# LayerNorm of the first query blocks on the finished residual tiles, with its modulation sums and the down-projection preparation in other slots

## The chip, the cores and the metric

The kernel runs on one core of a Trainium2 chip. The metric is the device time of one execution in microseconds. The core has a matrix engine (TensorE, PE in the profile; PEld is its weight load), VectorE (DVE), ScalarE (ACT), GpSimd (POOL), and SyncE (SP), which issues nearly all DMAs of this kernel from one queue in program order.

## The reference

A transformer block with modulation from a condition vector `c`, for 2048 rows of 512 features; 32 query heads, 8 key and value heads of 128, a window of the last 512 cached positions.

```
mod = silu(c) @ w_mod                     # six rows: sa, ca, ga, sb, cb, gb
h = layernorm(x) * (1 + ca) + sa
x = x + ga * attention(h, k_cache, v_cache, wq, wo)
h = layernorm(x) * (1 + cb) + sb
x = x + gb * ((gelu(h @ w_gate) * (h @ w_up)) @ w_down)
```

The change concerns the second `layernorm` (with `cb` and `sb`) for the first 1024 of the 2048 rows, that is for eight tiles of 128 rows.

## The kernel before

All matrix products are done in float16 with each operand split into a high and a low part, so one product is three matmuls (`mm3`, lines 86 to 88). The rows are cut into 16 tiles of 128, four tiles make a query block of 512, and two blocks make a half. A first stage of 512 steps does the attention: half 0 (blocks 0 and 1) in steps 0 to 255, half 1 in steps 256 to 511. A step takes one tile of one head: the scores (`scores`), the row maximum on VectorE (`peak`, L899), the exponential on ScalarE (`expo`, L908), and, two and three steps later, the high part on ScalarE (`high`, L920) and the low part on VectorE (`low`, L925), which SP then transposes by DMA into `pt`. Two PSUM banks hold the scores, so the scores of a step need the exponential of the step two before. Between the scores of two steps TensorE does three groups of other products from a list: query projections, probabilities times values (`po`), and the output projection (`py`), which VectorE adds into the residual tile `acc` (L876). After step 511 a second stage does the gated feed-forward part.

Everything else is hung on this loop by step numbers. `at(t, fn)` runs a function at the end of step t, `at(("w", t), fn)` after the loads of that step; `sched(pos, (load, steps))` plans a load three steps ahead of its first use and the steps at their slots. Loads planned so share five buffers of the tag `raw` in turn, which a planner at the end of the function counts through; `spare` moves planned loads and stores into steps without a DMA. Instructions of one engine run in the order in which the steps record them.

When a tile of half 0 has got its last output projection (`attn_final`, L882), the tile is stored to DRAM as `y1`, and three steps later its buffer is loaded with a tile of half 1. The second LayerNorm of the first eight tiles is generation 2 of `ln_tile` (L444): it is planned by `plan_gen(2, ...)` at steps 288, 299, 315, 326, 342, 353, 369 and 380. It reloads the tile from `y1` into a raw buffer (`xs`), takes mean and variance on VectorE (`bn_stats`, L376), a power on GpSimd (L386), normalizes on VectorE (L458), transposes on TensorE (L463), applies scale and shift on ScalarE (L471) into a tile `hf` from the six buffers `e` that the exponentials also use, stores it, and splits it into high (ScalarE, L483) and low (GpSimd, L485). Generation 3 (the other eight tiles) does the same in the second stage.

Scale and shift come from the modulation. For each of the six rows and four groups of 128 features, `mod_load` loads a 128x512 tile of weights (`wmc`) and `mod_col` forms one sum on VectorE (L135). Rows 3 and 4 are summed at slots 257 to 271, row 5 at slots 274 to 286; `mod_max` and `mod_scale` then turn rows 3 and 4 into scaled columns, at steps 272 and 274.

From step 286 on, every 27 steps, `prep_set` and `prep_wd` (L1262, L1301) prepare two sets of gate and up weights and two tiles of down-projection weights for the second stage: loaded, scaled and split on GpSimd into `stage` tiles (raw buffers too) and stored back. `prep_wd` starts 18 steps into each period.

Of the kernel before, what the change touches and what calls it, by code (L numbers as in the profile page):

```python
# [17 lines left out]
P = 128  # L18
# [45 lines left out]
def block_kernel(ctx: ExitStack, tc: tile.TileContext, x, kT, v, wq, wo, wg, wu, wd, cT, wc, wm, out):  # L64
# [379 lines left out]
    def ln_tile(gen, i, src):  # L444
        jsc, jsh = ln_cols("a" if gen < 2 else "f")
        qb, i = divmod(i % (2 * QT), QT)
        st = {}

        def load():
            st["x"] = raw("xs")  # L450
            dma(st["x"], src())

        def stat():
            ln_stat(st["x"], st)
            ln_power(st)

        def norm():
            nc.vector.tensor_scalar(st["x"], st["x"], st["mv"][:, 0:1], st["rs"], op0=ALU.subtract, op1=ALU.mult)  # L458

        def turn():  # L460
            st["ps"] = bank("acc", "pln", NACC)
            for dt in range(KT):
                nc.tensor.transpose(st["ps"][:, dt * P:(dt + 1) * P], st["x"][:, dt * P:(dt + 1) * P], ident)  # L463

        def affine(dts):
            if 0 in dts:
                st["f"] = tmp("hf")
            f = st["f"]
            for dt in dts:
                sl = slice(dt * P, (dt + 1) * P)  # L470
                nc.scalar.activation(f[:, sl], st["ps"][:, sl], AF.Identity,  # L471
                                     scale=cols[:, jsc, dt:dt + 1], bias=cols[:, jsh, dt:dt + 1])
            if KT - 1 in dts:
                dma(spilled(gen, qb)[:, :, i * P:(i + 1) * P], f.rearrange("p (k q) -> p k q", k=KT))

        def parts(act):
            o = slice(i * P, (i + 1) * P)
            f = st["f"].rearrange("p (k q) -> p k q", k=KT)
            for h, name in enumerate(("b11", "b21") if qb == 0 else (None, "b22")):
                if name:  # L480
                    t, src = block(gen, name), f[:, 2 * h:2 * h + 2, :]
                    if act:
                        nc.scalar.activation(t[:, 0:2, o], src, AF.Copy)  # L483
                    else:
                        nc.gpsimd.tensor_tensor(t[:, 2:4, o], src, t[:, 0:2, o], op=ALU.subtract)  # L485

        more = [lambda: parts(True), lambda: parts(False)] if gen < 3 else []
        return load, [stat, norm, turn, lambda: affine((0, 1)), lambda: affine((2, 3))] + more
# [393 lines left out]
    def attn_final(ti):  # L882
        y1[ti] = dram.tile([P, D], F32, name=f"y{ti}")
        dma(y1[ti], acc[ti])
        nxt = (ti + 2 * QT) % NT
        at(now[0] + 3, lambda: load_acc(nxt, rows_of(x, nxt) if ti < 2 * QT else y1[nxt]))

    def scores(t):
        u, i = divmod(t, 4)
# [188 lines left out]
    for dt in range(KT):  # L1078
        sched(6 + dt, (lambda dt=dt: gate_load(dt), [lambda dt=dt: gate_cols(dt)]), ahead=8)
    at(("d", 10), lambda: ts(cols[:, 2, :], gps["ps"][:, 0:KT], 1.0, None, ALU.mult))  # L1080
    for j, ts_ in ((3, (257, 261, 265, 269)), (4, (259, 263, 267, 271)), (5, (274, 278, 282, 286))):
        for dt in range(KT):
            box = {}
            sched(ts_[dt], (lambda box=box, j=j, dt=dt: box.update(f=mod_load(j, dt)), [lambda box=box: box["f"]()]))
    at(11, lambda: mod_row(2))
    mx = {}
    at(("w", 272), lambda: mx.update(m=mod_max(3)))
    at(274, lambda: mod_scale(3, "mf", 1.0, mx["m"]))

    def sched_combos(gen, p, base):  # L1090
        for k, (load, steps) in enumerate(combos(gen, p, nc.gpsimd if gen or p == 0 else nc.vector, False, 0 if gen else 1 if p else 2, 0 if gen or p else 5)):
# [18 lines left out]
            sched_combos(gen, p, t_cb + dcb * p)  # L1110

    plan_gen(1, [78 + 16 * i for i in range(8)], 201, 33, lambda i: rows_of(x, 2 * QT + i))
    plan_gen(2, [T // 2 + 32 + 27 * (i // 2) + 11 * (i % 2) for i in range(8)], 478, 10, lambda i: y1[i])

    def store_set(key, k):
        store(("w", key, k), SET[key][k])
# [214 lines left out]
    for n in range(NP):  # L1331
        b = T // 2 + 30 + 27 * n
        prep_set(2 * n, b)
        prep_set(2 * n + 1, b + 13)
        prep_wd(n, b + 18)
    for k in range(2):
        at(T - 1 + 2 * k, lambda k=k: WO.update({("f", 0, k): fetch(("wd", 0, k), get_wo())}))
    for q, ps_ in ((0, (T - 18, T - 17, T - 16, T - 15)), (1, (T - 8, T - 7, T - 3, T)), (2, (T + 2, T + 3, T + 4, T + 5))):
# [228 lines left out]
```

## Time and profile before

| | us |
|---|---|
| median of three runs | 1769.49 |
| lowest, highest | 1769.39, 1770.97 |
| the profiled execution | 1767.57 |
| its span, first to last instruction | 1765.8 |
| TensorE busy | 1730.5 |
| VectorE busy | 1442.3 |
| ScalarE busy | 1210.3 |
| GpSimd busy | 875.9 |

The granted TensorE clock was 1.000 over the span. Rows of the timeline give the start in us, the length, the engine, the line, the operation, output and inputs, and in brackets how long the engine stood idle before it and what ended that. Rows by stretch give the stretch, its length, and then busy time and number of instructions for PE, PEld, DVE, ACT and POOL, the granted clock, the busy share of the DMA engines and GB/s. Rows of a tile give the count and the shortest, median and longest duration in ns, with the start of the first and the last in us. Rows of groups give busy time in us and the mean in ns, then the idle time of the engine before them. Rows of waits give the sum in us, how often, and the longest.

### The profile page before, as it was taken

The numbers are of one execution on the slowest core, as the hardware profiler recorded it, in microseconds if no ns is written. First come the engines' busy times: TensorE is split into PE (matmuls) and PEld (weight loads), VectorE is DVE, ScalarE is ACT, GpSimd is POOL, SyncE is SP. The second block draws the span as 40 slices with busy tenths as digits, with TensorE's granted clock in tenths as the row PEclk, the third lists the DMA queues.
The fourth block names the chain that finished last, engine by engine and source line by source line (L and its number), as shares of the span: only waits on it lengthen the run. The fifth ranks groups of instructions, "written<-read, shape, count | busy, mean of one in ns | idle before, by whom it ended". The sixth has DMA issues, their size and how long they took to land.

```text
span 1765.8 us, 25953 instructions
## 1 busy us (share of the span) xinstructions
PE 1730.5 (98%) x8112; PEld 796.0 (45%) x8114; DVE 1442.3 (82%) x2517; ACT 1210.3 (69%) x2814; POOL 875.9 (50%) x1095
## 2 busy tenths in 40 slices
PE   7899999999999999999999999999999999999999
PEld 5444444444444444444444444444444444444443
DVE  7888888888888888988888888888885867766676
ACT  6887787878778777677878777777773455434342
POOL 4879878776788872235475465565520033000000
PEclk9999999999999999999999999999999999999999
DMA  7999998999999989998999999999985543252222
GB/s 230 211 196 212 214 217 200 223 203 219 217 217 229 205 186 196 205 225 200 236 205 219 234 214 200 223 207 208 198 171 141 182 146 111 69 188 75 86 75 75
DMA packets 663273, 329.71 MB, mean 187 GB/s; under 512 B 553184, under 2 KB 575968, under 8 KB 663136
## 3 DMA queue, kind: packets, MB, share of 16 engines
q1 hardware_dynamic: 662848, 327.53, 80.2%
q8 instruction: 64, 1.05, 0.2%
q14 instruction: 73, 0.60, 0.1%
q10 hardware_dynamic: 288, 0.52, 0.1%
HBM read 133.83 MB, written 59.90 MB: 110 GB/s over the span
## 4 chain that ended last, share of the span: by engine, by line
PE 76%; DVE 11%; ACT 5%; POOL 3%; issue 3%; DMA 2%; SPq 0%; POOLq 0%; ACTq 0%; DVEq 0%
PE py L86 7%; PE py L87 7%; PE py L88 7%; PE ps L86 5%; PE ps L88 5%; PE ps L87 5%; PE po L86 4%; PE po L87 4%; PE po L88 4%; DVE p L925 3%; PE fa L86 3%; PE fa L88 2%; PE fa L87 2%; DVE nm L899 2%; PE qa L86 2%
## 5 line engine op out<-in xcount | busy, mean ns | idle before, releaser
L908 ACT ACTIVATE ee<-ps,nm 128x512 f32<-128x512 f32 x512 | 351.2, 686 | 254.1 <-DVE nm L899 244.4
L925 DVE SCALAR_TENSOR_TENSOR p<-ee,rr,p 128x512 f16<-128x512 f32 x512 | 463.4, 905 | 0.2
L899 DVE TENSOR_REDUCE nm<-ps 128x1 f32<-128x512 f32 x512 | 348.8, 681 | 73.5 <-PE ps L88 72.0
L920 ACT ACTIVATE p<-ee,rr 128x512 f16<-128x512 f32 x512 | 365.2, 714 | 1.7 <-DMA pt<-p 1.4
L86 PE MATMUL ps<-k,qt 128*128 128x512 f16 x512 | 194.1, 379 | 16.5 <-DVE qt L668 13.1
L86 PE MATMUL py<-wo,ot 128*128 128x512 f16 x512 | 194.1, 379 | 1.6 <-DVE ot L668 1.6
L86 PE MATMUL po<-pt,v 128*128 128x512 f16 x512 | 194.1, 379 | 0.1
L87 PE MATMUL po<-pt,v 128*128 128x512 f16 x512 | 194.0, 379 | 0.0
L88 PE MATMUL po<-pt,v 128*128 128x512 f16 x512 | 194.0, 379 | 0.0
L87 PE MATMUL py<-wo,ot 128*128 128x512 f16 x512 | 194.0, 379 | 0.0
L88 PE MATMUL py<-wo,ot 128*128 128x512 f16 x512 | 194.0, 379 | 0.0
L88 PE MATMUL ps<-k,qt 128*128 128x512 f16 x512 | 194.0, 379 | 0.0
L87 PE MATMUL ps<-k,qt 128*128 128x512 f16 x512 | 193.9, 379 | 0.0
L916 DVE RECIPROCAL rr<-rr 128x2 f32<-128x2 f32 x256 | 41.5, 162 | 102.7 <-ACT rr L913 101.3
L386 POOL TENSOR_TENSOR rs<-rs,nhalf 128x1 f32<-128x1 f32 x32 | 19.6, 611 | 194.1 <-DVE rs L380 191.5
L86 PEld LDWEIGHTS <-w 128*128 128x128 f16 x728 | 71.2, 98 | 88.4 <-DMA w<-kept 2.9
L87 PEld LDWEIGHTS <-w 128*128 128x128 f16 x728 | 71.2, 98 | 87.3 <-issue 2.7
L88 PEld LDWEIGHTS <-w 128*128 128x128 f16 x728 | 71.2, 98 | 86.0 <-issue 0.2
L876 DVE SCALAR_TENSOR_TENSOR acc<-py,dysc,acc 128x512 f32<-128x512 f32 x112 | 81.6, 746 | 28.8 <-PE py L88 28.0
L876 DVE SCALAR_TENSOR_TENSOR acc<-py,ysc,acc 128x512 f32<-128x512 f32 x128 | 94.6, 739 | 10.9 <-PE py L88 10.9
L908 ACT ACTIVATION_READ_ACCUMULATOR ee<-ps,nm 128x1 f32 x512 | 100.7, 197 | 0.0
L668 DVE SCALAR_TENSOR_TENSOR ot<-po,ot 128x512 f16<-128x512 f32 x128 | 86.9, 679 | 0.0
(263 smaller groups left out, 3817.1 us busy)
## 6 DMA issues: line engine op xcount, KB each, us to landing
w<-kept SPq DMA_DIRECT2D x123, 256.0 KB, 3.2
wo<-kept SPq DMA_DIRECT2D x60, 256.0 KB, 3.6
raw<-in_wo SPq DMA_DIRECT2D x56, 256.0 KB, 3.2
kept<-stage SPq DMA_DIRECT2D x56, 256.0 KB, 3.4
kept<-w SPq DMA_DIRECT2D x39, 256.0 KB, 3.4
rw<-in_wq SPq DMA_DIRECT2D x38, 256.0 KB, 3.3
hs<-hf SPq DMA_DIRECT2D x32, 256.0 KB, 2.7
pt<-p SPq DMA_TRANSPOSE x512, 3.5
```

Source lines behind the costliest of these rows:

```text
L86: nc.tensor.matmul(ps, llo, rhi, start=first, stop=False, skip_group_check=chain)
L87: nc.tensor.matmul(ps, lhi, rlo, start=False, stop=False, skip_group_check=chain)
L88: nc.tensor.matmul(ps, lhi, rhi, start=False, stop=last, skip_group_check=chain)
L386: nc.gpsimd.tensor_tensor(st["rs"], st["rs"], nhalf, op=ALU.pow)
L668: return lambda: nc.vector.scalar_tensor_tensor(t[:, 1, :], src, scale, t[:, 0, :], op0=ALU.mult, op1=ALU.subtract)
L876: nc.vector.scalar_tensor_tensor(acc[ti], st["p"], by, acc[ti], op0=ALU.mult, op1=ALU.add)
L899: nc.vector.tensor_reduce(nm, E[t]["ps"], axis=AX.X, op=ALU.max, negate=True)
L908: nc.scalar.activation(e, E[t]["ps"], AF.Exp, bias=E[t]["nm"], scale=1.0, accum_out=sm[:, t % 2:t % 2 + 1])
L916: return lambda: nc.vector.reciprocal(r, r)
L920: nc.scalar.activation(p16[:, 0, :], E[t]["e"], AF.Copy, scale=E[t]["r"])
L925: nc.vector.scalar_tensor_tensor(p16[:, 1, :], E[t]["e"], E[t]["r"], p16[:, 0, :], op0=ALU.mult, op1=ALU.subtract)
```

## The change

For generation 2, `ln_tile` works on the residual tile itself: no reload, the statistics are taken from `acc`, GpSimd forms minus mean times the reciprocal deviation (`nmean`), and the norm is one ScalarE activation in place where it was a VectorE operation. `hf` is taken from the raw buffers, without being known to the planner. The steps hang on `attn_final`: statistics one step after a tile is finished, norm six, transposes eight, scale and shift nine and ten, parts twelve and thirteen steps after. The load of the next tile into the same buffer moves from three to twelve steps after. The sums of rows 3 and 4 move to slots 211 to 229, and their maximum and scale to steps 232 and 234. `prep_wd` starts 21 steps into each period where it was 18. The combinations of generation 2 stay at steps 478 and 488.

```diff
--- before.py
+++ after.py
@@ -447,14 +447,22 @@
         st = {}
 
         def load():
-            st["x"] = raw("xs")
-            dma(st["x"], src())
+            if gen == 2:
+                st["x"] = src()
+            else:
+                st["x"] = raw("xs")
+                dma(st["x"], src())
 
         def stat():
             ln_stat(st["x"], st)
             ln_power(st)
+            if gen == 2:
+                st["nm"] = small.tile([P, 1], F32, name="nmean")
+                pool_ts(st["nm"], st["mv"][:, 0:1], st["rs"], -1.0)
 
         def norm():
+            if gen == 2:
+                return nc.scalar.activation(st["x"], st["x"], AF.Identity, bias=st["nm"], scale=st["rs"])
             nc.vector.tensor_scalar(st["x"], st["x"], st["mv"][:, 0:1], st["rs"], op0=ALU.subtract, op1=ALU.mult)
 
         def turn():
@@ -464,7 +472,7 @@
 
         def affine(dts):
             if 0 in dts:
-                st["f"] = tmp("hf")
+                st["f"] = raw("hf") if gen == 2 else tmp("hf")
             f = st["f"]
             for dt in dts:
                 sl = slice(dt * P, (dt + 1) * P)
@@ -883,7 +891,14 @@
         y1[ti] = dram.tile([P, D], F32, name=f"y{ti}")
         dma(y1[ti], acc[ti])
         nxt = (ti + 2 * QT) % NT
-        at(now[0] + 3, lambda: load_acc(nxt, rows_of(x, nxt) if ti < 2 * QT else y1[nxt]))
+        if ti < 2 * QT:
+            own, steps = ln_tile(2, ti, lambda: acc[ti])
+            own()
+            for d, fn in zip((1, 6, 8, 9, 10, 12, 13), steps):
+                at(("w", now[0] + d), fn)
+            at(now[0] + 12, lambda: load_acc(nxt, rows_of(x, nxt)))
+        else:
+            at(now[0] + 3, lambda: load_acc(nxt, y1[nxt]))
 
     def scores(t):
         u, i = divmod(t, 4)
@@ -1078,14 +1093,14 @@
     for dt in range(KT):
         sched(6 + dt, (lambda dt=dt: gate_load(dt), [lambda dt=dt: gate_cols(dt)]), ahead=8)
     at(("d", 10), lambda: ts(cols[:, 2, :], gps["ps"][:, 0:KT], 1.0, None, ALU.mult))
-    for j, ts_ in ((3, (257, 261, 265, 269)), (4, (259, 263, 267, 271)), (5, (274, 278, 282, 286))):
+    for j, ts_ in ((3, (211, 215, 223, 227)), (4, (213, 217, 225, 229)), (5, (274, 278, 282, 286))):
         for dt in range(KT):
             box = {}
             sched(ts_[dt], (lambda box=box, j=j, dt=dt: box.update(f=mod_load(j, dt)), [lambda box=box: box["f"]()]))
     at(11, lambda: mod_row(2))
     mx = {}
-    at(("w", 272), lambda: mx.update(m=mod_max(3)))
-    at(274, lambda: mod_scale(3, "mf", 1.0, mx["m"]))
+    at(("w", 232), lambda: mx.update(m=mod_max(3)))
+    at(234, lambda: mod_scale(3, "mf", 1.0, mx["m"]))
 
     def sched_combos(gen, p, base):
         for k, (load, steps) in enumerate(combos(gen, p, nc.gpsimd if gen or p == 0 else nc.vector, False, 0 if gen else 1 if p else 2, 0 if gen or p else 5)):
@@ -1110,7 +1125,8 @@
             sched_combos(gen, p, t_cb + dcb * p)
 
     plan_gen(1, [78 + 16 * i for i in range(8)], 201, 33, lambda i: rows_of(x, 2 * QT + i))
-    plan_gen(2, [T // 2 + 32 + 27 * (i // 2) + 11 * (i % 2) for i in range(8)], 478, 10, lambda i: y1[i])
+    for p in range(2):
+        sched_combos(2, p, 478 + 10 * p)
 
     def store_set(key, k):
         store(("w", key, k), SET[key][k])
@@ -1332,7 +1348,7 @@
         b = T // 2 + 30 + 27 * n
         prep_set(2 * n, b)
         prep_set(2 * n + 1, b + 13)
-        prep_wd(n, b + 18)
+        prep_wd(n, b + 21)
     for k in range(2):
         at(T - 1 + 2 * k, lambda k=k: WO.update({("f", 0, k): fetch(("wd", 0, k), get_wo())}))
     for q, ps_ in ((0, (T - 18, T - 17, T - 16, T - 15)), (1, (T - 8, T - 7, T - 3, T)), (2, (T + 2, T + 3, T + 4, T + 5))):
```

## The prediction

> **What bounds the kernel now.** I read the page first, then the busy time by stretches, then in order of time the places where TensorE stands still.
>
> ```profile
> span 1765.8 us, 25953 instructions
> PE 1730.5 (98%) x8112; PEld 796.0 (45%) x8114; DVE 1442.3 (82%) x2517; ACT 1210.3 (69%) x2814; POOL 875.9 (50%) x1095
> PE 76%; DVE 11%; ACT 5%; POOL 3%; issue 3%; DMA 2%; SPq 0%; POOLq 0%; ACTq 0%; DVEq 0%
> ```
>
> TensorE works 98% of the span and carries 76% of the chain that ended last. The change neither adds nor removes a matmul or a transpose, so only TensorE's idle time can change. The rows below give, by stretch, the length and then the busy time of PE, PEld, DVE, ACT and POOL.
>
> ```profile
> 560.00:620.00 60.00, 59.45 (x279) 26.77 (x277) 50.35 (x92) 46.53 (x116) 53.12 (x70) 1.00 0.97 213
> 640.00:650.00 10.00, 9.37 (x44) 4.12 (x43) 8.44 (x12) 6.51 (x17) 6.40 (x7) 1.00 0.75 179
> 680.00:720.00 40.00, 40.00 (x187) 18.09 (x186) 37.67 (x75) 28.56 (x68) 7.39 (x8) 1.00 0.94 211
> 720.00:740.00 20.00, 18.97 (x89) 8.67 (x88) 18.37 (x34) 12.75 (x31) 11.73 (x14) 1.00 0.84 177
> 740.00:790.00 50.00, 50.00 (x238) 23.25 (x237) 43.40 (x83) 38.63 (x94) 14.86 (x20) 1.00 1.00 226
> 820.00:840.00 20.00, 19.10 (x89) 8.15 (x87) 18.05 (x33) 14.56 (x37) 16.10 (x20) 1.00 0.87 204
> 870.00:890.00 20.00, 20.00 (x98) 9.39 (x97) 17.42 (x34) 17.59 (x44) 10.26 (x15) 1.00 1.03 220
> 900.00:910.00 10.00, 9.19 (x44) 4.01 (x42) 8.29 (x15) 6.94 (x17) 6.70 (x7) 1.00 1.02 255
> 970.00:980.00 10.00, 9.00 (x44) 4.01 (x42) 8.73 (x16) 5.92 (x16) 5.67 (x6) 1.00 1.00 238
> 1010.00:1260.00 250.00, 250.00 (x1172) 113.69 (x1171) 209.48 (x366) 191.43 (x465) 144.05 (x183) 1.00 0.98 212
> ...
> 500.00:1300.00 800.00, 794.26 (x3716) 361.43 (x3714) 687.62 (x1211) 613.76 (x1491) 464.38 (x565) 1.00 0.96 212
> ```
>
> Between 500 and 1300 us, where everything is that the change touches, TensorE idles only 800.00 - 794.26 = 5.74 us. That caps any gain here at 0.32% of the span. The idle time stands in few places: 0.55 us (560:620), 0.63 (640:650), 1.03 (720:740), 0.90 (820:840), 0.81 (900:910) and 1.00 (970:980). VectorE is 94% busy in 680:720 and TensorE still has no gap there, so a full engine is not a stop by itself; a late row maximum is. The next rows show the stop at 732 us and those at 908 and 977.
>
> ```profile
> 727.17 0.38 PE L194 MATMUL pst<-ident,mm 128*128 128x128 f32 x2
> 728.59 0.41 DVE L196 TENSOR_REDUCE mg<-pst 128x2 f32<-128x256 f32 x1
> 730.31 0.68 DVE L135 SCALAR_TENSOR_TENSOR wmc<-wmc,sbc 128x512 f32<-128x512 f32 x1
> 730.92 0.68 DVE L899 TENSOR_REDUCE nm<-ps 128x1 f32<-128x512 f32 x1
> 731.63 0.69 ACT L908 ACTIVATE ee<-ps,nm 128x512 f32<-128x512 f32 x1 [4.09 <-DVE nm L899]
> 732.46 0.38 PE L86 MATMUL ps<-k,qt 128*128 128x512 f16 x1 [1.03 <-ACT ee L908]
> ...
> 906.00 0.67 DVE L376 BATCH_NORM_STATS2 bn<-xs 128x6 f32<-128x512 f32 x1
> 907.71 0.69 ACT L908 ACTIVATE ee<-ps,nm 128x512 f32<-128x512 f32 x1 [2.66 <-DVE nm L899]
> ...
> 974.84 0.69 DVE L376 BATCH_NORM_STATS2 bn<-xs 128x6 f32<-128x512 f32 x1 [1.20 <-DMA xs<-y]
> ```
>
> At 728 the scale of the modulation (mod_scale) and a modulation sum stand on VectorE ahead of the maximum nm; the exponential comes late, its score bank is not free, and TensorE loses 1.03 us. At 906 and 975 the LayerNorm statistics of a reloaded tile take that place, the second time after 1.20 us of waiting for the reload.
>
> **The change part by part.** The profiled execution took 1767.57 us, its span and 1.77 us around it; the median of the runs is 1769.49, 1.92 above it. The sum goes against 1767.57 and the 1.92 are added at its end. These rows place and price the moved work.
>
> ```profile
> L135 DVE SCALAR_TENSOR_TENSOR wmc<-wmc,sbc x12: 676/682/1093, 684.6 to 758.6; 128x512 f32<-128x512 f32 x12
> DMA to landing us min/median/max: 2.9/3.3/4.6
> ...
> L94 SPq DMA_DIRECT2D y<-acc x16: 319/529/643, 688.7 to 1370.9; - x16
> L405 ACT ACTIVATE xn<-acc,nmean x2: 721/722/722, 7.7 to 8.7; 128x512 f32<-128x512 f32 x2
> ...
> L376 DVE BATCH_NORM_STATS2 bn<-xs x24: 660/680/695, 228.8 to 1429.6; 128x6 f32<-128x512 f32 x24
> L458 DVE TENSOR_SCALAR xs<-xs,mv,rs x24: 533/540/548, 235.7 to 1431.9; 128x512 f32<-128x512 f32 x24
> L94 SPq DMA_DIRECT2D xs<-y x16: 331/406/646, 758.0 to 1426.3; - x16
> ...
> 779.47 0.81 ACT L471 ACTIVATE hf<-pln,cols 128x128 f32<-128x128 f32 x2
> 782.38 0.81 ACT L471 ACTIVATE hf<-pln,cols 128x128 f32<-128x128 f32 x2
> 784.44 0.73 ACT L483 ACTIVATE b<-hf 128x256 f16<-128x256 f32 x2
> ...
> L386 POOL TENSOR_TENSOR rs<-rs,nhalf 128x1 f32<-128x1 f32 x32 | 19.6, 611 | 194.1 <-DVE rs L380 191.5 <-DVE nmean L383 2.6
> ```
>
> The twelve sums run at steps 257 to 286 and lie between 684.6 and 758.6 us, so a step is about 2.55 us; slots 211 to 229 are about 567 to 613 us, slot 234 about 626.
>
> 1. *LayerNorm taken out of 758 to 1000 us.* Eight reloads of 256 KB, eight statistics, norms, transposes and affines leave this region, and a landing can no longer hold VectorE. The three stops fall away: 0.90 + 0.81 + 1.00 = 2.71 us. The reason to expect all of it: the down-projection tiles are prepared every 27 steps (69 us) and go on after the LayerNorm has ended, and in 1010:1260 TensorE has 250.00 busy of 250.00. If the stops belong to that preparation alone, the gain is 0.
>
> 2. *mod_scale from step 274 to 234.* The 1.03 us at 732 go. At 234 the same chain runs with no sum behind it (0.68 us less), so it costs at least about 1.03 - 0.68 = 0.35; the combinations of the second query blocks begin beside it and 640:650 already has 0.63 idle, so at most 1.03 + 0.63 = 1.66. I take 1.0: the same chain, the neighbouring row.
>
> 3. *Eight sums at 567 to 613 us.* Each is 0.68 us on VectorE when GpSimd rests, 1.09 in the one case that met it; eight are 5.4 to 8.7 us. VectorE has 60.00 - 50.35 = 9.65 us idle in 560:620, so they fit, but leave 1.0 to 4.2. The lower price is 0 (680:720 holds 94% with no gap); the upper is one stop like the one at 732 for each group of four, 2.06. I take 0.8, below the middle, because 680:720 is the same instruction at the same spacing. Their loads go out three steps ahead (7.6 us) and land in 2.9 to 4.6, as before.
>
> The port is where a page speaks against this. The row has twelve sums with a median of 682 ns and one of 1093, and that one, the first at 684.6 us, is the one beside GpSimd work. The Trainium skill, page "SBUF — State Buffer", section "Who interferes with whom", says that a VectorE instruction with two SBUF inputs contends with a GpSimd instruction that reads SBUF, and that the later one waits out the earlier. The trace agrees: 1093 against 682. By that rule all eight sums would take the long price in 560:620, where GpSimd is 53.12 of 60 busy; that is the second rival below.
>
> 4. *LayerNorm in place at 689 to 793 us.* The finished tiles appear about every four steps (10.2 us) from 688.7 on, so eight LayerNorms now follow each other where they stood 11 to 16 steps apart. ScalarE gets per tile 0.81 + 0.81 + 0.73 from the rows, and the norm, which VectorE did in 0.54; the nearest ScalarE row is L405, the same shape from the same tile, 0.72. That is 3.07 per tile, 2.7 with the one high part of the second block. Over 680 to 790 ScalarE is 28.56 + 12.75 + 38.63 = 79.94 busy of 110; seven tiles more (one lies there already) bring about 21 us: 101 of 110, 92%. VectorE was 37.67 + 18.37 + 43.40 = 99.44; it loses eight sums and mod_scale (about 7.5) and gains about seven statistics of 1.0, so it stays. GpSimd gets eight small products (each under the 0.61 of its power) and the low parts, and is only 33.98 of 110 busy; its weight sets now queue behind each tile's statistics. Nothing in SP's queue waits longer: each store follows its affine as before, and the loads of the next x tiles, nine steps later, are first needed at about step 290.
> Bounds: 0 from the tile at 764 to 786, which ran without a gap in 740:790, and from 870:890, where ScalarE has 17.59 of 20 and TensorE 20.00; above, every tile stops TensorE as long as the dearer of those at 900 and 820, 8 x 0.90 = 7.2. I take 0.1 per tile, 0.8, since the nearest rows show none and this load is only somewhat higher.
>
> 5. *hf in the five raw buffers, and the preparation three slots later.* 0: with the reloads gone the raw queue has eight tenants fewer and eight other ones. What hides it is the lead of the transposed probabilities over their use; the longest such hold now is this one.
>
> ```profile
> SPq L94 <- POOL stage L157: 29.8, 15, 3.8
> ```
>
> SP stood up to 3.8 us behind GpSimd fifteen times in 780:1260, and TensorE never waited for a transpose. If that cover is gone, a stop costs about 1 us, the price of the others here.
>
> Sum: 1767.57 - 2.71 - 1.03 + 1.0 + 0.8 + 0.8 = 1766.4 profiled, and + 1.92 = **1768.4 us** as a median. With the lower ends, -2.71 - 1.03 + 0.35 = -3.4: 1766.1. With the upper ends, -3.74 + 1.66 + 2.06 + 7.2 = +7.2: 1776.7; without the gain of step 1, 2.7 more.
>
> **The rivals.**
>
> *ScalarE becomes the bound from 700 to 790 us (slower).* Eight tiles in a row at 92% leave no time to catch up, exponentials come late as at 732, and each tile costs 0.90: -1.1 + 6.4 = +5.3, so 1774.8. For it: 900:910 stops with ScalarE at only 6.94 of 10. Against it: 870:890. It decides where a tile's four steps hold more ScalarE work than 10.2 us; the base of 79.94 / 110 x 10.2 = 7.4 plus 3.07 is 10.5, a little over, though adjoining rows overlap by about 0.1 us each, which makes the true need smaller.
>
> *The sums meet GpSimd (slower).* At 1.09 each VectorE is at 50.35 + 8.7 = 59.1 of 60; if none of that finds idle time, 8.7 takes the place of 0.8: +6.8, so 1776.2. It decides when VectorE's idle time there, mostly waits for scores, is really the lead of TensorE. Against it: 680:720.
>
> *The stops belong to the down-projection preparation.* They stay at 820, 900 and 970: +2.7, so 1771.1. Against it: 1010:1260.
>
> *Both new places are free (faster).* The lower ends, and the reshuffled order also takes the 0.55 and 0.63 of 560:650: -4.6, so 1764.9.
>
> **How the numbers follow.** What a measurement of this kernel tells from no change is about 0.2%, 3.5 us; the bounds are 1765.95 and 1773.03. My forecast has 0.45, with its own range 1766.0 to 1771.0; the stops that stay 0.14 (within the bound too); ScalarE the bound 0.15; the sums on GpSimd 0.09; the free case 0.17. So faster 0.17, same 0.59, slower 0.24. The range of 1764.8 to 1774.8 takes in the free case and the middle of the ScalarE case and leaves out about 0.17, nearly all above.
>
> **What would show it.** Right: no reload of y tiles before 1300 us; no gap at 820 to 980; TensorE idle in 500:1300 between 3.5 and 6; eight LayerNorms between 689 and 793 with ScalarE near 92%; the sums at 567 to 613 above 0.68 us where GpSimd works. Wrong: scores waiting for ee in 700:790 by more than 2 us in sum, sums followed by late maxima at 567 to 626, or TensorE waiting for pt. The end beyond 1300 us should be the same; a difference there would be one that I have no step for.

## The result, and the profile after

The changed kernel took 1775.83 us (median of 6 runs, 1774.93 to 1778.80) beside 1769.68 us for the kernel before in the same series: 1.0035 times as long, 95% interval 1.0025 to 1.0046. A second series (the last experiment) gave 1.0027 (1.0018 to 1.0036). The prediction was 1768.4 us and no change.

The profiled execution took 1774.93 us. Its page begins with the span, the busy time of each engine and the chain that ended last:

```profile
span 1773.1 us, 25974 instructions
PE 1734.3 (98%) x8114; PEld 796.1 (45%) x8114; DVE 1449.5 (82%) x2509; ACT 1215.7 (69%) x2822; POOL 877.8 (50%) x1103
PE 70%; DVE 14%; ACT 8%; issue 3%; DMA 2%; POOL 2%; SPq 0%; ACTq 0%; POOLq 0%; DVEq 0%
```

The chain gave 6 points of TensorE away, three each to VectorE and ScalarE. Where, the table by stretch shows. The columns are the length, then busy time (and instructions) of PE, PEld, DVE, ACT and POOL, the granted clock, the DMA share and GB/s. First the changed kernel:

```profile
560.00:640.00 80.00, 76.24 (x353) 33.89 (x351) 74.38 (x140) 58.23 (x142) 65.07 (x79) 1.00 0.97 219
640.00:660.00 20.00, 18.16 (x85) 8.08 (x84) 17.09 (x26) 15.45 (x38) 14.34 (x14) 1.00 0.85 213
690.00:740.00 50.00, 50.00 (x240) 23.46 (x238) 43.81 (x80) 39.21 (x94) 19.95 (x26) 1.00 0.88 191
740.00:800.00 60.00, 57.46 (x278) 27.21 (x277) 49.53 (x96) 53.12 (x132) 27.05 (x37) 1.00 0.92 201
800.00:1010.00 210.00, 210.00 (x983) 95.28 (x982) 182.76 (x309) 160.71 (x390) 116.92 (x151) 1.00 0.96 212
...
500.00:1300.00 800.00, 789.50 (x3692) 358.98 (x3691) 691.38 (x1197) 614.99 (x1489) 467.63 (x576) 1.00 0.95 208
```

and the same stretches of the kernel before, in the same view:

```profile
560.00:640.00 80.00, 79.44 (x371) 35.80 (x369) 68.33 (x120) 62.04 (x152) 68.30 (x82) 1.00 0.98 212
640.00:660.00 20.00, 19.37 (x90) 8.61 (x89) 17.89 (x27) 14.20 (x35) 15.67 (x17) 1.00 0.83 168
690.00:740.00 50.00, 48.97 (x228) 22.25 (x227) 46.63 (x94) 34.99 (x82) 12.81 (x14) 1.00 0.93 201
740.00:800.00 60.00, 60.00 (x284) 27.76 (x283) 52.67 (x101) 46.94 (x115) 16.58 (x22) 1.00 1.02 233
800.00:1010.00 210.00, 207.29 (x976) 94.88 (x975) 179.87 (x320) 164.14 (x405) 124.42 (x162) 1.00 0.96 217
```

TensorE's idle time rose by 3.20 us in 560:640 (0.56 to 3.76) and by 1.21 in 640:660, fell by 1.03 in 690:740, rose by 2.54 in 740:800, and fell by 2.71 in 800:1010. Over 500:1300 it went from 5.74 to 10.50 us. Behind each rise stand single stops of TensorE. The longest, in the timeline of the changed kernel, with start and duration of each, with the idle time ahead of it and what ended that in brackets:

```profile
603.59 1.62 DVE L135 SCALAR_TENSOR_TENSOR wmc<-wmc,sbc 128x512 f32<-128x512 f32 x1
605.82 1.66 DVE L940 SCALAR_TENSOR_TENSOR p<-ee,rr,p 128x512 f16<-128x512 f32 x1
608.13 0.39 PE L86 MATMUL py<-wo,ot 128*128 128x512 f16 x1 [1.70 <-DVE ot L676]
656.40 0.39 PE L86 MATMUL ps<-k,qt 128*128 128x512 f16 x1 [1.84 <-DVE qt L676]
746.74 0.66 PE L471 MATMUL pln<-ident,acc 128*128 128x128 f32 x4 [0.80 <-ACT hf L479]
774.72 0.81 ACT L479 ACTIVATE hf<-pln,cols 128x128 f32<-128x128 f32 x2
775.65 0.17 DVE L931 RECIPROCAL rr<-rr 128x2 f32<-128x2 f32 x1 [1.44 <-ACT rr L928]
777.13 0.39 PE L86 MATMUL py<-wo,ot 128*128 128x512 f16 x1 [1.01 <-DVE ot L676]
791.23 0.66 PE L471 MATMUL pln<-ident,acc 128*128 128x128 f32 x4 [0.73 <-ACT hf L479]
1278.30 0.39 PE L86 MATMUL ps<-k,qt 128*128 128x512 f16 x1 [1.58 <-DVE qt L676]
```

A sum takes 1.62 us instead of 0.68 and the low half of the probabilities behind it 1.66. Behind both on VectorE stands `ot`, the attention result that the output projection (`py`) needs, and it comes 1.70 us late. At 656 (step 242) `qt`, the queries of the next scores, is late. At 747 and 791 the transposes of a LayerNorm tile wait for the affine (the scale and shift that write `hf`) of the tile before. At 777 `ot` is late again: on ScalarE an affine stands ahead of the softmax factor `rr`, and VectorE waits 1.44 us for it. At 1278 (step 486) `qt` is late. In the kernel before, the stops answering those at 656 and 1278 are short:

```profile
648.16 0.39 PE L86 MATMUL ps<-k,qt 128*128 128x512 f16 x1 [0.63 <-DVE qt L668]
...
1270.87 0.39 PE L86 MATMUL ps<-k,qt 128*128 128x512 f16 x1 [0.20 <-DVE qt L668]
```

**A part that is not the change.** The profiled spans differ by 7.3 us, but 2.4 of that is there by 200 us, where both kernels run the same program. The changed kernel's profile has a low granted clock in two places (rows of the columns as above, PE alone: length, busy, clock, DMA share, GB/s):

```profile
66.00:68.00 2.00, 0.89 (x4) 0.97 0.17 36
68.00:70.00 2.00, 2.00 (x6) 0.50 1.08 259
70.00:72.00 2.00, 2.00 (x9) 0.68 0.84 202
...
86.00:88.00 2.00, 0.14 (x1) 1.00 1.07 185
88.00:90.00 2.00, 2.00 (x7) 0.59 1.02 240
90.00:92.00 2.00, 2.00 (x7) 0.56 0.25 94
```

The kernel before has 1.00 in all of these stretches in its profile. Whether that belongs to the change is taken up below. Without it the traces differ by about 5 us, and the named terms add up to 3.20 + 1.21 - 1.03 + 2.54 - 2.71 + 1.38 (the stop at 1278, 1.58 against 0.20) = **+4.6 us**, a ratio of 1.0026, inside both intervals. About 0.3 us stays unnamed.

### The profile page after: what moved, and what is told of

Read it like the earlier page. It is cut to its first block, busy times and chain, and to the rows that moved or that the text cites. A ratio compares the mean times of both kernels' runs of the same rounds, so it can differ in the third digit from the quotient of the medians.

```text
span 1773.1 us, 25974 instructions
## 1 busy us (share of the span) xinstructions
PE 1734.3 (98%) x8114; PEld 796.1 (45%) x8114; DVE 1449.5 (82%) x2509; ACT 1215.7 (69%) x2822; POOL 877.8 (50%) x1103
## 3 DMA queue, kind: packets, MB, share of 16 engines
q8 instruction: 64, 1.05, 0.3%
## 4 chain that ended last, share of the span: by engine, by line
PE 70%; DVE 14%; ACT 8%; issue 3%; DMA 2%; POOL 2%; SPq 0%; ACTq 0%; POOLq 0%; DVEq 0%
PE py L86 7%; PE py L87 7%; PE py L88 7%; DVE p L940 4%; PE ps L86 4%; PE ps L88 4%; PE ps L87 4%; PE po L86 4%; PE po L88 4%; PE po L87 4%; DVE nm L914 3%; PE fa L86 3%; PE fa L88 2%; PE fa L87 2%; ACT ee L923 2%
## 5 line engine op out<-in xcount | busy, mean ns | idle before, releaser
L940 DVE SCALAR_TENSOR_TENSOR p<-ee,rr,p 128x512 f16<-128x512 f32 x512 | 469.3, 917 | 0.8 <-ACT p L935 0.7
```

Source lines behind the costliest of these rows:

```text
L940: nc.vector.scalar_tensor_tensor(p16[:, 1, :], E[t]["e"], E[t]["r"], p16[:, 0, :], op0=ALU.mult, op1=ALU.subtract)
```

## The experiments

Theory 1: the sums beside a busy GpSimd, and the LayerNorm in dense order, make the loss; its rivals are given with each run. The diffs are in short form, each with the kernel that it starts from. "Idle" is TensorE's idle time from the table by stretch in 560:640, 640:660 and 690:800: before 0.56, 0.63, 1.03; changed 3.76, 1.84, 2.54. Ratios are to the kernel before in the same series. The expectations reckon a stop from the starts of the matmuls, which makes it about 0.17 us longer than the brackets of the rows (1.43 for 1.26).

| run | median us | ratio (95%) | idle |
|---|---|---|---|
| e1_sums_only | 1773.99 | 1.0022 (1.0013-1.0031) | 3.63, 1.62, 0.12 |
| e2_sums_quiet | 1770.33 | 1.0000 (0.9991-1.0009) | 0.87, 0.63, 3.02 |
| e3_wd18 | 1773.56 | 1.0019 (1.0010-1.0028) | 4.04, 1.73, 2.57 |
| e4_one_input | 1770.72 | 1.0002 (0.9993-1.0011) | 1.48, 1.86, 2.57 |
| e5_dve_alone | 1772.65 | 1.0011 (1.0002-1.0019) | 2.08, 0.64, 3.42 |
| e6_loads_alone | 1768.10 | 0.9988 (0.9979-0.9997) | 0.82, 0.64, 3.09 |
| e7_spaced_wd18 | 1779.40 | 1.0052 (1.0039-1.0065) | 0.28, 0.65, 8.46 |
| e8_norm_dve | 1771.05 | 1.0004 (0.9995-1.0013) | 0.59, 0.64, 4.19 |
| e9_scale_late | 1774.30 | 1.0026 (1.0015-1.0036) | 3.80, 0.76, 2.82 |
| e10_quiet_wd18 | 1768.39 | 0.9991 (0.9982-1.0000) | 0.36, 0.68, 3.04 |
| e11_turn_late | 1773.26 | 1.0020 (1.0010-1.0030) | 0.63, 0.64, 5.59 |
| e12_hf_tmp | 1769.21 | 0.9995 (0.9986-1.0004) | 0.34, 0.64, 3.04 |
| e13_affine_x | 1769.20 | 0.9992 (0.9983-1.0000) | 0.25, 0.64, 2.23 |
| e14_affine_once | 1768.72 | 0.9994 (0.9985-1.0002) | 0.61, 0.64, 1.96 |
| e15_affine_once6 | 1769.48 | 0.9992 (0.9982-1.0001) | 0.75, 0.64, 1.63 |
| e16_after_again | 1775.06 | 1.0027 (1.0018-1.0036) | 4.26, 1.85, 2.53 |

e16 is the changed kernel once more: two profiles of one kernel differ by up to 0.5 us in such a stretch (3.76 and 4.26), so smaller differences of a stretch say little; a single stop repeats better (1.70 us at 608 in both).

**The sums alone, and the sums elsewhere.** e1 takes the kernel before and moves only sums and scale; e2 takes the changed kernel and moves its sums to where GpSimd is quiet.

```diff
 e1, against before
-    (3, (257, 261, 265, 269)), (4, (259, 263, 267, 271))   maximum 272, scale 274
+    (3, (211, 215, 223, 227)), (4, (213, 217, 225, 229))   maximum 232, scale 234
 e2, against the changed kernel
-    (3, (211, 215, 223, 227)), (4, (213, 217, 225, 229))   maximum 232, scale 234
+    (3, (245, 247, 253, 255)), (4, (249, 251, 257, 259))   maximum 261, scale 263
```

> The kernel before with one part of the change: the eight modulation sums at steps 211 to 229 and the scale at 234; LayerNorm stays on the reloaded tiles. Theory 1 (the sums meet GpSimd): TensorE loses the 4.4 us in 560:660 that it loses in the changed kernel (idle 0.55 + 0.63 before, 5.6 after), and gets 1.03 us back at 732; so +3.4 us against the kernel before, some 1773, with stops that wait for VectorE's ot and qt near 606 and 654 us and sums above 1 us. Rival A (the dense LayerNorm is the cause, the sums only looked late because the LayerNorm's order shifted them): no more than 0.55 + 0.63 idle in 560:660, and 1.03 gained, so -1.0, some 1768.5. Rival B (a low granted clock at 60 to 100 us is the cause and belongs to the changed kernel): clock 1.00 there in this run and no difference to the kernel before.

> The changed kernel with its eight sums at steps 245 to 259, the maximum at 261 and the scale at 263, where GpSimd is busy 6 to 7 us of 20; LayerNorm in place stays as it is. Theory 1: the 4.4 us of 560:660 go, the sums are back at 0.68 us; one stop of about 1 us may come at the scale; so about 3.4 to 4.4 us under the changed kernel, 1771.5 to 1772.5. Rival A (dense LayerNorm is the cause): no gain, 1775 to 1776, with the stops between 740 and 800 us as in the changed kernel. Rival B (clock at 60 to 100 us): no gain while the clock there is below 0.95, or a gain of 2.4 us where it is 1.00, whatever the sums do.

e1 lost 0.22%, some 4 us, with 3.63 and 1.62 us idle; the sums and their scale make that loss without any LayerNorm in place. e2 is level with the kernel before; of its eight sums two are long (1.09 us at 662 and 1.16 at 682), and no stop follows them. The view of tile `wmc` in e2 for 640:690 (its count, shortest, median and longest ns, first and last start; the eighth sum, 0.69 us, starts at 692):

```profile
L135 DVE SCALAR_TENSOR_TENSOR wmc<-wmc,sbc x7: 678/679/1156, 657.3 to 686.6; 128x512 f32<-128x512 f32 x7
```

Rival A falls with e1, rival B with e2, whose profile has the low clock (0.89 in 60:70) and is still about 5 us under the changed kernel.

**One input, the instruction alone, the loads alone.** What is it about the sums? e4 lets each sum read one tile in SBUF and so leaves out the product with the activated condition; e5 and e6 put back into e2, at the old slots, VectorE's part or the loads' part.

```diff
 e4, against the changed kernel, for j in (3, 4)
-        nc.vector.scalar_tensor_tensor(src, src, 1.0, by, op0=ALU.mult, op1=ALU.mult, accum_out=c)
+        nc.vector.tensor_scalar(src, src, 1.0, 0.0, op0=ALU.mult, op1=ALU.add, accum_out=c)
 e5, against e2, at steps 211, 213, 215, 217, 223, 225, 227, 229
+        nc.vector.scalar_tensor_tensor(sbc, sbc, 1.0, sbc, op0=ALU.mult, op1=ALU.max)
 e6, against e2, at the same steps
+        sched(t_, (lambda k_=k_: mod_load(3 + k_ % 2, k_ // 2), [nop]))
```

> The changed kernel, where the eight sums at steps 211 to 229 read one tile in SBUF (the weights alone are summed; the multiplication with the activated condition is left out, so the modulation of the second LayerNorm is not the reference's). Same slots, same loads, same scale. Theory 1, by contention with GpSimd: a sum takes about 0.7 us or less beside GpSimd where the two-input form took 1.1 to 1.64, and most of the 4.4 us of 560:660 go (3 to 4 us under the changed kernel). Rival C (VectorE has no slack there whatever the sums take, 0.68 each is too much already): the sums take 0.68, but the stops near 606 and 654 us stay and the time falls by under 1.5 us.

> e2_sums_quiet (1770.33, TensorE idle 0.87 + 0 + 0.63 us in 560:620, 620:640, 640:660) with eight extra instructions on VectorE at steps 211 to 229: two-input, 128x512 f32, in place on the resident condition tile (its value does not change), no load and no accumulator read. The real sums stay at 245 to 259. Theory 1a (two causes: VectorE meets GpSimd at 567 to 613 us, and the loads of the sums push other loads back in SP's queue): the extra instructions take 1.1 to 1.64 us beside GpSimd, the stop at 606 us comes back (1.0 to 1.9 us), the one at step 242 (654 us) stays at 0.8; 2 to 2.5 us over e2. Theory 1b (the port alone): both stops come back, 4 us over e2. Theory 1c (the loads alone): nothing comes back.

> e2_sums_quiet with the eight loads alone at the slots 211 to 229 (the same weights a second time into the raw buffers, nothing reads them), the real sums at 245 to 259. Theory 1a: the three loads of the combination tiles go out in a bunch 5 to 7 us later than in e2, GpSimd waits about 3.6 us for them, and the stop at step 242 is back at 1.8 to 2.0 us (0.8 in e2), while no stop over 0.6 us comes at 606; 1 to 1.7 us over e2. Theory 1b (the port alone): nothing over e2. Theory 1c (the loads alone): all 4 us.

The sums of the changed kernel in 560:640, from its view of tile `wmc`:

```profile
L135 DVE SCALAR_TENSOR_TENSOR wmc<-wmc,sbc x8: 675/864/1639, 571.3 to 620.8; 128x512 f32<-128x512 f32 x8
```

The same sums of e4, one input each:

```profile
L136 DVE TENSOR_SCALAR_CACHE_REDUCE wmc<-wmc x8: 668/671/675, 570.9 to 617.4; 128x512 f32<-128x512 f32 x8
```

The added instructions of e5, from its view of tile `sbc`:

```profile
L1101 DVE SCALAR_TENSOR_TENSOR sbc<-sbc x8: 677/1069/1641, 571.3 to 618.9; 128x512 f32<-128x512 f32 x8
```

With one input the eight take 0.67 us each; with two, in the same slots, with the same loads and beside the same GpSimd work, four take 1.05 to 1.64. So it is the second input that meets GpSimd. The Trainium skill, page "SBUF — State Buffer", section "Who interferes with whom", states both halves: two SBUF inputs contend with a GpSimd instruction that reads SBUF; at most one, outside the two-port modes, does not. Both agree with these rows. Of the 3.20 us in 560:640, 2.28 go with the one-input form (3.76 to 1.48); the 0.92 that stay over the kernel before are near the 0.8 of the prediction. e5 adds 1.21 us there and one stop, though another one, at 611 us and not at 606. Five of its eight are long (1.05 to 1.64), but ahead of the late `qt` VectorE itself stands waiting for a small product of GpSimd (`lt`). From e5's timeline:

```profile
610.57 0.16 DVE L263 RECIPROCAL lr<-lt 128x1 f32<-128x1 f32 x1 [1.26 <-POOL lt L237]
611.44 0.39 PE L86 MATMUL ps<-k,qt 128*128 128x512 f16 x1 [1.59 <-DVE qt L676]
```

e6 adds no stop. So the loads alone cost nothing and the instruction alone 1.2 of the 2.9 us between e2 (0.87) and the changed kernel (3.76). The other 1.7 comes only with loads and sums together. With both, the instructions stand at slightly other times against GpSimd's, and the sums bring small instructions that e5 leaves out (eight reads of the accumulator of 0.08 us, four additions of 0.15); which of these makes the 1.7 is not shown.

The medians move more than the rows. e4 lies 4 to 5 us under the changed kernel. e6 lies 0.12% under the kernel before, with an interval that leaves out 1, though its idle time in 500:1300 is 6.07 us against 5.74; among executions with the same mean clock of 0.998 it is 1769.06 against 1770.93, so the low clock does not explain it. That stays open.

What theory 1a expected of e6 fell: its combination loads did go out in a bunch, but the stop at step 242 stayed at 0.64. The cause of that stop was neither the two-input instructions nor the loads.

**The scale.** That stop was long in e1, e4 and the changed kernel, which have the scale at 234, and short in e2, e5 and e6. So e9 moves the maximum and the scale alone.

```diff
 e9, against the changed kernel
-    at(("w", 232), lambda: mx.update(m=mod_max(3)))
-    at(234, lambda: mod_scale(3, "mf", 1.0, mx["m"]))
+    at(("w", 261), lambda: mx.update(m=mod_max(3)))
+    at(263, lambda: mod_scale(3, "mf", 1.0, mx["m"]))
```

> The changed kernel with the maximum and the scale at 261 and 263; the sums stay at 211 to 229. The stop at step 242 (654 us) was 1.8 to 2.0 us in every kernel with both the sums' loads and the scale at 234, and 0.8 in those with the scale at 263, though one of them had the loads too. Theory 2 (the scale at 234 takes VectorE's lead, which is paid at step 242): the stop at 242 falls to about 0.8, so 1.0 to 1.2 us under the changed kernel, and 606 us keeps its 1.9. Rival (the sums that hold raw buffers, and so the late loads of the combination tiles): the stop stays at 1.8 to 2.0 and the time is that of the changed kernel.

From e9's timeline:

```profile
608.07 0.39 PE L86 MATMUL py<-wo,ot 128*128 128x512 f16 x1 [1.70 <-DVE ot L676]
654.99 0.39 PE L86 MATMUL ps<-k,qt 128*128 128x512 f16 x1 [0.63 <-DVE qt L676]
```

The stop at 606 us is untouched, the one at 242 is back at the kernel before's 0.63. The scale at 234 costs no stop where it stands; it takes VectorE's lead (the time by which VectorE is ready before TensorE is), and that is paid eight steps later. The lead can be seen where the row maximum `nm` waits for the scores. From the waits of VectorE in 626:656, that of e9 for the scores, and below it the only one that the changed kernel has:

```profile
DVE nm L914 <- PE ps L88: 1.6, 3, 0.8
...
DVE rr L931 <- ACT rr L928: 3.6, 5, 1.4
```

In e9 the maximum waits for the scores three times, in the changed kernel never: there VectorE runs behind. The rows decide here; the median of 1774.30 cannot be told from the changed kernel.

**The preparation three slots earlier again.**

```diff
 e3, against the changed kernel; e10, against e2
-        prep_wd(n, b + 21)
+        prep_wd(n, b + 18)
```

> The changed kernel with the preparation of the down-projection tiles back in its old slots (three steps earlier). Theory 1: the later slots cost only the longer stop at step 486 (1.75 us against 0.37), so at best 1.4 us under the changed kernel; the stops of 740:800 stay. Rival: the preparation in its old slots meets the raw buffers that hold the LayerNorm results, and the stops in 690:1000 become more: over 1 us slower than the changed kernel.

> e2_sums_quiet with the down-projection preparation in its old slots and nothing else. It splits e7_spaced_wd18, which lost 9 us over e2. Theory 2 (the spacing alone did that: LayerNorm steps shifted by one step stand in front of qt at the start of a unit): the stops of e2 in 690:800 (1.43, 1.19, 0.90) are unchanged, the one at step 486 falls from 1.76 to 0.4; about 1.3 us under e2, a little under the kernel before (ratio 0.999 to 1.000). Rival (the old slots of the preparation clash with the LayerNorm in place once the sums stand at 245 to 259): stops after the transposes as in e7, over 3 us above e2.

From e10's timeline:

```profile
1271.08 0.39 PE L86 MATMUL ps<-k,qt 128*128 128x512 f16 x1 [0.28 <-DVE qt L676]
```

In e3 (0.27) as in e10 the stop at step 486 is short again, and no stop over 0.3 us came in its place; the later slots cost 1.3 us and gave nothing. That price hangs on the rest of the order too: in e6 and e9, which keep the later slots, the stop is 0.78 and 0.99. e10's ratio is 0.9991, and its interval reaches 1.0000: not told apart from the kernel before.

**What the LayerNorm in place costs.** e2 and e10 still have the three stops of 740:800, some 3 us. Is ScalarE too full, or do single instructions stand badly? e8 takes eight norms of 0.82 us off ScalarE; e7 and e11 keep crowded tiles apart; e12 takes `hf` out of the raw buffers.

```diff
 e8, against e2 (and without the product that forms nmean)
-            if gen == 2:
-                return nc.scalar.activation(st["x"], st["x"], AF.Identity, bias=st["nm"], scale=st["rs"])
 e7, against e10: all steps of a LayerNorm, and the next load, from b: at least four steps behind the one before
+            b = lnt[0] = max(now[0], lnt[0] + 4)
 e11, against e10: c = 1 where the tile before was finished three steps ago
+            for d, fn in zip((1, 6, 8 + c, 9 + c, 10 + c, 12 + c, 13 + c), steps):
 e12, against e10
-                st["f"] = raw("hf") if gen == 2 else tmp("hf")
+                st["f"] = tmp("hf")
```

> e2_sums_quiet with the in-place norm on VectorE (as the reloaded tiles had it, 0.54 us) and not on ScalarE (0.82), and so without the small product on GpSimd. Theory 1 (the stops in 740:800 are the order of a few ScalarE instructions, the affines, and not a full ScalarE): the stops shrink by 0 to 1 us in sum, as the affines get 0.8 us more room per tile; within 1.5 us of e2. Rival (ScalarE is the bound from 700 to 790 us): ScalarE loses 6.6 us of work and all three stops (1.43 + 1.19 + 0.90) go, 3 to 3.5 us under e2.

> e2_sums_quiet with at least four steps between the LayerNorms of two tiles (tiles that are finished after three steps start one step later) and the down-projection preparation in its old slots. Theory 1: the two stops where the transposes wait for hf of the tile before (1.43 at 740 and 0.90 at 785 us) fall to under 0.2 each, the stop at step 486 falls from 1.76 to 0.4; 3.2 to 3.7 us under e2, 1766.5 to 1767.2, and 2.5 to 3.5 under the kernel before. Rival (ScalarE has too much work between 690 and 790 us, the spacing only moves the wait): stops of the same sum appear as late exponentials or late ot, no more than 1.4 us under e2.

> e10_quiet_wd18 with the transposes, affines and parts (not the statistics and the norm) of the two tiles that are finished after three steps one step later. Theory 2: the two stops where the transposes wait for hf (1.43 and 0.90) go, the statistics stay where they are, and so no new stop at qt; 2 us under e10, the fastest so far. Rival (any instruction one step later in the unit stands in front of qt, on TensorE or ScalarE too): stops of 0.7 to 1.6 us after these two transposes, no gain.

> e10_quiet_wd18 with the affine results of the in-place LayerNorm in the buffers of the exponentials (where the reloaded tiles had them) and not in the raw buffers. By the prediction's step 5 the raw buffers cost nothing, so what is to be seen is what they save: an hf tile is held for four steps and its store, one of six exponential buffers; theory 2: each of eight tiles delays one exponential by 0 to 0.9 us, so 0 to 5 us over e10. Rival (the raw buffers are the scarcer ones and hf delays the loads of the preparation): under e10 by 0.5 to 2 us.

e8 is no faster; its idle time in 690:800 rose from 3.02 to 4.19, with 86.42 of 110 busy on ScalarE against 92.12. A lighter ScalarE does not help here. e8 alone does not clear ScalarE, since the norms now load VectorE (99.36 against 95.96); but the stop that waits for `hf` grew in it from 1.26 to 1.74 us, and e14 below removes both such waits with ScalarE as busy as in e10.

e7 and e11 were misses: keeping tiles apart did not remove the stops but made larger ones. e10 splits e7: the spacing did it, not the preparation. Which step of a LayerNorm stands ahead of `qt` is seen in e7's timeline:

```profile
740.30 0.80 ACT L479 ACTIVATE hf<-pln,cols 128x128 f32<-128x128 f32 x2
740.98 0.82 ACT L465 ACTIVATE acc<-acc,nmean,rs 128x512 f32<-128x512 f32 x1
741.93 0.17 DVE L934 RECIPROCAL rr<-rr 128x2 f32<-128x2 f32 x1 [1.67 <-ACT rr L931]
744.11 0.39 PE L86 MATMUL ps<-k,qt 128*128 128x512 f16 x1 [1.59 <-DVE qt L676]
```

An affine and a norm stand on ScalarE ahead of the softmax factor `rr`; VectorE waits for it, and the low half and `qt` come after. In 690:800 these waits sum to 18.5 us in e7 and 11.6 in e10. In e11 the delayed tile comes within three steps of the next one, whose transposes wait 1.82 us. Both have one stop of about 3 us (2.82 in e7), which e11's timeline names:

```profile
798.22 0.81 ACT L479 ACTIVATE hf<-pln,cols 128x128 f32<-128x128 f32 x2 [5.18 <-POOL b L493]
799.75 0.38 PE L86 MATMUL ps<-k,qt 128*128 128x512 f16 x1 [3.03 <-ACT ee L927]
```

ScalarE waits 5.18 us for GpSimd's low part (`b`, L493) of an earlier tile, as the raw buffer that `hf` takes is still read. So the raw buffers do have an edge; in the changed kernel's order it isn't reached, and e12, which is e10 without them, differs by nothing that can be measured. Neither e7 nor e11 was tried without them.

e13, e14 and e15 move single affines of e10.

```diff
 e13: the second affine ahead of the step's products
+                at(("x" if d == 10 else "w", now[0] + d), fn)
 e14: both affines of tiles 3 and 7 in one step
+            for d, fn in zip((1, 6, 8, 9, 9 if k in (3, 7) else 10, 12, 13), steps):
 e15: also those of tile 6 a step later (c = k == 6), hf as in e12
+            for d, fn in zip((1, 6, 8, 9 + c, 9 if k in (3, 7) else 10 + c, 12 + c, 13 + c), steps):
```

> e10_quiet_wd18 with the second affine of each tile ahead of the step's products on ScalarE and not behind them (same step). Theory 2 (order): the affine is done up to 0.7 us earlier, so the two stops of the transposes fall from 1.44 and 0.91 to about 0.7 and 0.2; the 0.8 us stand ahead of other ScalarE work in each of eight steps and may cost some of it again; 0 to 1.4 us under e10. Rival (load): the sum of the stops in 690:800 stays at 3.5 us or grows.

> e10_quiet_wd18 with both affines of the third and the seventh tile in one step (the second one a step earlier); the other tiles as they were. Theory 2 (order): the bank is free one step (2.55 us) earlier, both stops of the transposes (1.44 and 0.91) go; one exponential may come 0.8 us later, hidden by what TensorE has queued; 1.5 to 2.3 us under e10. Rival (load): 1.6 us of affines in one step make the next exponential late, and stops of 0.6 to 0.9 us (score after ee) take their place; no gain.

> As e14_affine_once, and the affines and parts of the sixth tile one step later, and hf in the exponentials' buffers (no difference by e12). Theory 2 (order): the stop at 770 us (1.21), where the sixth tile's affine stands ahead of the softmax factors, goes too; 2.5 to 3.5 us under e10, about 1765 to 1766, and 0.25% under the kernel before. Rival: the affine one step later stands ahead of something else that TensorE waits for, and the stop of 1 us only moves.

In e14 both waits of the transposes are gone, and two short waits for an exponential and a longer one for `ot` stand in their place, from its timeline:

```profile
748.55 0.38 PE L86 MATMUL ps<-k,qt 128*128 128x512 f16 x1 [0.41 <-ACT ee L926]
759.66 0.38 PE L86 MATMUL ps<-k,qt 128*128 128x512 f16 x1 [0.16 <-ACT ee L926]
771.50 0.39 PE L86 MATMUL py<-wo,ot 128*128 128x512 f16 x1 [1.39 <-DVE ot L676]
```

The idle time of 690:800 fell from 3.04 (e10) to 2.23, 1.96 and 1.63 us; in e15 the stop ahead of `ot` is 0.69. Neither side is right alone: the order sets which stop comes, and a quarter to nearly half of the idle time can be taken away so; the rest moves. In e13 the gain comes back as a stop of 1.33 us at 803.63, where TensorE waits for transposed probabilities. No median shows a gain: the three ratios lie between 0.9992 and 0.9994 beside e10's 0.9991, and e15, expected at 1765 to 1766, took 1769.48. No version tried is certainly faster than the kernel before: only e6's interval lies under 1 (its upper end is 0.9997), and no row shows where that gain would come from.

**The changed kernel again, for the clock.**

> The changed kernel once more, unchanged. By the stops, it is 4.6 to 5.0 us slower than the kernel before where both ran at the same clock between 60 and 100 us, so 1774.5 to 1775.5 beside a median of 1769.5 to 1770.5 (ratio 1.0026 to 1.0029). Rival (the low clock at 60 to 100 us belongs to the changed kernel): the ratio stays at 1.0035 or above.

It gave 1.0027, the terms' own size. The interval reaches 1.0036, so the ratio alone does not refute the rival; the profiles do. The low clock in 60:100 came in the profiles of seven kernels in both places (changed, e2, e4, e9, e11, e12, e16), in five in one (e1, e5, e6, e14, e15), and in six not at all (before, e3, e7, e8, e10, e13): all run the same program there. And it comes to the kernel before as well: of its 33 runs in the first series, three had a mean clock of 1.000 (median 1767.96 us) and 24 one of 0.998 or 0.997 (1770.23); the mean does not say where in the run the clock was low. So it does not belong to the change; the profile before was one of the few executions without it, the profile after a usual one. It is 2.4 us of the 7.3 between the two profiled spans and little of the difference of the medians.

## Why the prediction was wrong, step by step

Step 1 was right, and step 2 nearly so. Steps 3, 4 and 5 were too cheap, and step 3 failed most: it took the cost of the sums from a stretch where GpSimd rests.

1. *LayerNorm taken out of 758 to 1000 us, -2.71.* Right: 210.00 busy of 210.00 in 800:1010 (209.71 in e16), and 210.00 also with the preparation in its old slots (e3, e10). The rival that the stops belong to the preparation fell. The reading behind it covered less than went away: of the 0.81 in 900:910, 0.50 stand at 905.47, ahead of the statistics at 906.00, and wait for `qt`.
2. *mod_scale at 234, -1.03 + 1.0.* Both sizes right: 690:740 is full, and e9 puts the new cost at 1.2 (1.84 against 0.63). The prediction priced it as a stop at the scale itself, with 640:650 only in its upper bound; it is paid there, at step 242, as VectorE's lost lead.
3. *Eight sums at 567 to 613 us, +0.8.* The largest miss: 3.2. Here the step chose 680:720 as the nearest row, "the same instruction at the same spacing", though GpSimd is busy 7.39 of 40 there and 53.12 of 60 in the new place. The rival "the sums meet GpSimd" had the mechanism; its price of 6.8 supposed all eight long, and four were (1.05 to 1.64 us). The low half of the probabilities has two inputs as well and takes 1.66 behind a long sum. The kernel before could have shown the price: its low halves reach 1.34 us in 560:640, with a median of 0.77, and 1.57 at 640.38. With the one-input form (e4) the step costs 0.92, so what it left out is, nearly all, the contention. That the rival's 1776.2 lies near the result is chance, since other terms make up the rest.
4. *LayerNorm in place, +0.8.* 2.5, inside its bounds of 0 to 7.2. ScalarE was 92.33 busy of 110, 84% and not 92%: the affines, norms and high parts add 23.6 us in length, but rows overlap and fewer steps of attention fell into the stretch. e8 and e14 speak against its load as the cause. Not foreseen was the order: transposes of a tile that is finished three steps after the last one need a bank of PSUM before ScalarE has done the affine of the tile before (0.80 and 0.73), and one affine ahead of a softmax factor (1.01). The prediction looked for late exponentials, the price of the old stops, and took the average spacing of four steps for every tile. The rival "ScalarE becomes the bound" did not come: no stop in 740:800 waits for an exponential.
5. *hf in raw buffers 0, preparation 0.* hf right in this order (e12). The preparation's shift cost 1.4 at step 486 (1.58 against 0.20; e3 and e10 undo it, and in e6 and e9 it is smaller). The prediction looked at the probabilities' transposes as its cover, which held; the stop came through `qt`, beyond the stretch that step had looked at.

The terms' sum was -1.1 against the kernel before and is +4.6: 2.4 from step 3, 1.7 from step 4, 1.4 from step 5, 0.2 from step 2. TensorE's idle time in 500:1300 was to lie between 3.5 and 6 us and is 10.5 (11.1 in e16). The end beyond 1300 us is unchanged, as predicted: its largest stops are 0.90 and 1.52 us before, 0.90 and 1.53 after, each 7.3 to 7.4 us later. The 1.92 us between profile and median, added without a cause, are about the size of the low clock.

## What to carry to other kernels

When work moves, take its price from a row where the other engines are as busy as in the new place, not from one with the same instruction: the same two-input sum took 0.68 us beside an idle GpSimd and up to 1.64 beside a busy one. Where TensorE runs at 98%, a delay of VectorE need not show where it arises: look for the next step at which its lead is used up, and for the shortest spacing of a repeated step, not its mean. Before two profiled spans are subtracted, compare a stretch where both run the same program.

## What the runs showed of the chip that was not expected

A short stop can cost twice. In e7, after a stop of 2.82 us (the last matmul before it starts at 801.43, the next at 804.63), the clock fell, from its table by stretch, PE alone:

```profile
802.00:804.00 2.00, 0.00 (x0) 1.00 0.98 296
804.00:806.00 2.00, 1.37 (x6) 0.93 1.05 239
806.00:808.00 2.00, 2.00 (x6) 0.50 0.17 49
808.00:810.00 2.00, 2.00 (x9) 0.72 0.95 224
```

From 805.7 to about 809.1 us, some 3.4 us, matmuls came every 0.43 us instead of 0.215, which lost 1.7 us more. The same happens in 60:100 in 12 of the 18 profiles, in the changed kernel after pauses of TensorE of 2.69 and 2.78 us. The length of the pause does not decide it alone: in e11 a stop of 3.03 us left the clock at 1.00, and the kernel before has a pause of 2.68 us in the same place of its program, also at 1.00. The Trainium skill, page "TensorE: Matmul & The Clock Gate", section "What's actually happening", has the clock halve after an idle window of about 3.4 us and return after a busy one, and the window runs freely. The length of the slow time agrees; that the low clock comes after some pauses and not after others of the same length fits a free-running window, though no run here shows the window itself. A whole idle window was not needed: 2.82 us sufficed.

Contention also reaches work that was never moved: the low half of the probabilities takes 0.73 us beside a quiet GpSimd and 1.66 beside its products, right behind a long sum. It does so without the change as well (1.57 us at 640.38 in the kernel before).
